# A fused recurrent-attention and mixer kernel on one core: all operations in another order, with other PSUM banks and other constant matmuls

## The chip, the core and the metric

One core of a Trainium2 chip runs the kernel. The core has a matrix engine (TensorE; PE in the profile, with PEld for its weight loads), a vector engine (DVE), a scalar engine (ACT), a general one (GpSimd, POOL) and a sync engine (SP) that here does nothing but issue DMAs. Each engine works through its own queue in order. The metric is the device time of one execution in microseconds (us), as a median over executions; lower is better.

## The reference

The first half is a recurrence over 768 tokens for 4 batches with 8 heads of dimension 40; the second half mixes the result over tokens and channels.

```python
for t in range(S):                       # state: [B, H, D, D]
    y[:, :, t] = einsum('bhd,bhde->bhe', rt, state)
    Sa = einsum('bhde,bhe->bhd', state, at)
    state = state * wt[:, :, None, :] - einsum('bhd,bhe->bhde', Sa, bt) \
            + einsum('bhd,bhe->bhde', vt, kt)
x = y.transpose(0, 2, 1, 3).reshape(B, S, H * D)
theta = x @ w_theta
zr, zi = x * cos(theta), x * sin(theta)
u = x + einsum('ts,bsd->btd', w_tok_r, zr) + einsum('ts,bsd->btd', w_tok_i, zi)
out = u + maximum(u @ w_ch, 0)
```

Inputs and output are float32.

## The kernel before

The sequence is cut into chunks of 128 tokens: 6 for each batch, 24 in all, numbered i = 0 to 23. For each chunk the recurrence is written as matmuls: scores between the chunk's tokens, masked to a triangle, and a state that goes from chunk to chunk within a batch.

The program builds a list of 1,602 operations (`Plan`, L165). Each has a kind, a chunk number and an engine, and some have an alternative on another engine. The kinds that matter here:

- `lw`, `lk`, `lb`, `la`, `lv` (L442) and `loadr`, `loado` (L454): loads of 160 KB on SP, for one chunk, or halves of r and v for two chunks. The tiles that they fill are `raw_w`, `raw_kb`, `raw_a`, `raw_v`, `raw_r`, in rings of two to six.
- `ln`, `cs`, `cx`, `exp`, `ew`: the decay factors, by ACT and PE (constant triangles as weights).
- `kb` and `ah` (L462 on POOL, L461 on DVE): two products for k and b and one for a, each 128 x 320. `o`, `r`, `v`: casts. `tkb`, `ta`, `to`, `tr`, `tv`, `tb`, `nut`, `xt`, `ut`, `wt`: transposes on PE (L410, L414, L575, L578), each with an evacuation from PSUM (`ekb`, `ea` and so on) on ACT or DVE. Eleven of the transposes run on SP as DMAs.
- `spsi`, `sphi`, `slv`, `slu` (L609): score matmuls into two banks each; their masks `mpsi`, `mphi`, `mlv`, `mlu` are one product with a triangle on DVE (L618), or a copy on ACT (L620) followed by a selection `sel` on POOL (L622).
- `x0`, `nx`, `nu`, `enu`, `gt`, `egt`, `wgt`, `gd`, `egd`: the chain of the recurrence. `x0` (L650, L656) multiplies the old state, `nu` (L669) needs the masked phi, `gt` (L692) makes the new state, and from chunk 4 on it is finished by a sum on DVE (`egt`, L703) and a product on POOL (`wgt`, L707).
- `y`, `ex` (L844): the chunk's result x. `th`, `eth`, `sin` (L885), `z` (L899 on DVE, L900 on POOL), `row` (L916), `uadd` (L922), `ch`, `oo`, `st`: the mixer. A row needs z of all six chunks of its batch. `wdma` (L967, L995) are the loads of the mixer's weights, issued by POOL.

Dependencies between operations are kept by semaphores whatever the order. Four tables, written out at the head of the file by a planner that ran before, say the rest. `ORDER` is the order in which all operations are emitted, and so the order of each engine's queue. `HOMES` gives each PSUM tile its bank, in the order in which the tiles are opened; there are 8 banks, and an operation that opens a bank waits for the last reader of what was there. `PICK` lists operations that run on their alternative engine, or whose transposes go into two banks rather than one. `WARM` maps an operation to a bank and a number n: ahead of that operation, n matmuls of a constant tile `busy` with itself are issued into that bank (L1044); nothing reads them.

```python
for o in plan.order():
    if o.idx in WARM:
        at, n = WARM[o.idx]
        for _ in range(n):
            nc.tensor.matmul(banks[:, at, 0:128], lhsT=busy[:, 0:128], rhs=busy[:, 0:128], ...)
    ...
    if o.fn is not None:
        o.fn()
```

In the order before, the first entries of the queues are these (bank behind @, d for two banks, W for constant matmuls):

```
PE    W25 cs0@7 cx0@1 W1 to0@4 W4 ta0@0d W8 tkb0@0d tb0@5d spsi0@0d W11 tr0@2d cx1@7 cs1@6
      cs2@4 cx2@1 x0_0@5 sphi0@2d slv1@6d nu0 slv0@2d ta1 tkb1 gt0 tb1 nut0 spsi1 ...
DVE   ah0 kb0 eb0 mpsi0 nx0 mphi0 ah1 mlv0 egt0 eb1 kb2 kb2 mphi1 ...
POOL  o0 kb0 r0 wdma kb1 kb1 sel1 wdma o2 ah2 ...
SP    lw0 loado0 lk0 loado0 la0 loado2 lb0 loadr0 lw1 loadr0 lw2 lb1 lk1 la1 la2 lk2 ...
```

and around chunks 10 to 12:

```
POOL  ... kb11 kb11 ah11 wgt9 wdma kb12 wdma ah12 kb12 wdma wgt10 wdma wdma v12 ...
SP    ... (73) lk12 la11 lw13 la12 loadr12 (78) lb12 lv12 lw14 loadr12 ...
```

Of the kernel before, what the change touches and what calls it, by code (L numbers as in the profile page):

```python
# [26 lines left out]
    0, 6, 1, 7, 3, 18, 20, 2, 21, 5, 23, 22, 32, 8, 24, 25, 33, 4, 12, 27, 30, 10, 31, 34, 26,  # L27
    35, 9, 28, 36, 40, 29, 37, 11, 69, 58, 44, 45, 46, 119, 15, 41, 72, 43, 70, 120, 42, 122,
    13, 71, 98, 73, 47, 99, 75, 87, 48, 49, 19, 74, 88, 14, 76, 100, 53, 89, 50, 101, 123, 51,
    52, 79, 77, 80, 57, 90, 121, 102, 78, 38, 103, 131, 106, 39, 81, 107, 54, 124, 126, 82, 108,  # L30
    104, 125, 129, 84, 83, 130, 17, 132, 109, 85, 86, 56, 127, 134, 156, 110, 128, 16, 137, 157,
    133, 146, 55, 184, 105, 143, 147, 158, 138, 187, 96, 185, 159, 111, 144, 145, 186, 152, 164,
    148, 234, 135, 160, 136, 92, 61, 165, 189, 237, 139, 161, 166, 112, 213, 188, 97, 167, 168,
    59, 214, 140, 91, 238, 190, 235, 141, 215, 191, 93, 162, 236, 169, 163, 60, 194, 142, 170,
    62, 192, 95, 195, 149, 193, 216, 267, 240, 299, 217, 150, 94, 196, 246, 218, 153, 302, 197,
    198, 303, 239, 247, 210, 202, 249, 199, 208, 241, 203, 271, 200, 201, 219, 242, 212, 248,
    63, 204, 272, 244, 205, 64, 243, 221, 273, 220, 245, 171, 254, 211, 222, 274, 258, 172, 261,
    155, 151, 259, 279, 262, 263, 223, 154, 174, 280, 300, 260, 250, 224, 225, 173, 251, 281,
    301, 320, 175, 496, 255, 304, 282, 283, 275, 256, 325, 177, 226, 349, 276, 206, 497, 257,
    176, 264, 498, 306, 268, 227, 352, 265, 284, 499, 327, 305, 285, 277, 326, 328, 309, 278,  # L40
    317, 310, 329, 207, 318, 319, 353, 307, 330, 286, 269, 356, 308, 350, 331, 287, 500, 361,
    311, 332, 539, 252, 270, 336, 312, 313, 253, 359, 333, 351, 314, 360, 362, 354, 337, 209,
    315, 316, 540, 364, 338, 363, 386, 266, 541, 387, 288, 382, 339, 340, 388, 289, 355, 290,
    389, 291, 116, 321, 357, 390, 341, 412, 502, 358, 391, 323, 365, 501, 542, 292, 373, 342,
    392, 367, 366, 503, 374, 375, 376, 368, 517, 504, 411, 181, 506, 377, 378, 524, 414, 505,
    334, 393, 322, 525, 369, 507, 394, 395, 526, 335, 508, 418, 527, 383, 528, 509, 510, 554,
    396, 370, 415, 543, 397, 511, 371, 324, 529, 113, 532, 372, 117, 512, 513, 533, 546, 398,
    118, 572, 384, 595, 514, 178, 603, 573, 550, 399, 530, 515, 516, 413, 596, 385, 551, 534,
    597, 574, 544, 531, 182, 598, 642, 400, 535, 536, 575, 417, 401, 183, 402, 521, 576, 403,
    545, 581, 404, 577, 379, 599, 114, 582, 547, 555, 115, 380, 381, 600, 548, 556, 557, 583,  # L50
# [12 lines left out]
    741, 65, 882, 672, 757, 778, 408, 755, 736, 450, 779, 753, 451, 737, 673, 780, 742, 883,
    452, 682, 781, 453, 884, 683, 764, 885, 669, 782, 758, 765, 783, 454, 455, 759, 784, 346,
    456, 767, 785, 786, 457, 766, 458, 459, 773, 743, 796, 405, 768, 769, 460, 787, 760, 802,
    443, 744, 912, 797, 788, 724, 444, 343, 461, 798, 761, 887, 913, 445, 789, 763, 446, 462,
    762, 886, 914, 790, 463, 770, 723, 915, 347, 448, 888, 771, 791, 348, 792, 793, 800, 920,
    890, 794, 795, 409, 921, 891, 889, 916, 905, 410, 892, 801, 805, 917, 464, 406, 893, 918,
    772, 344, 407, 465, 896, 804, 345, 899, 728, 922, 803, 897, 898, 480, 725, 481, 808, 482,
    955, 483, 900, 901, 473, 811, 474, 927, 484, 923, 485, 799, 919, 726, 960, 806, 466, 928,  # L70
    961, 924, 475, 727, 929, 486, 894, 962, 895, 476, 907, 963, 477, 933, 930, 983, 819, 906,
    932, 467, 931, 807, 468, 1030, 969, 902, 469, 970, 478, 809, 903, 471, 908, 820, 984, 479,
    821, 810, 934, 822, 985, 777, 971, 942, 986, 487, 936, 972, 973, 488, 964, 935, 1086, 774,
    823, 904, 937, 824, 1031, 825, 938, 1032, 775, 489, 965, 925, 939, 1033, 490, 966, 926, 940,
    776, 491, 949, 941, 1036, 492, 943, 1034, 946, 950, 951, 945, 812, 1035, 957, 947, 813, 814,
    815, 1037, 494, 944, 1087, 958, 967, 987, 974, 968, 948, 1088, 1039, 975, 956, 1041, 1040,
    816, 1089, 988, 817, 1042, 1014, 818, 1007, 976, 991, 1015, 952, 977, 826, 1090, 989, 1016,
    953, 954, 827, 996, 911, 1017, 1052, 990, 992, 997, 909, 1023, 993, 1053, 1054, 1018, 1092,
    1058, 994, 1024, 978, 995, 979, 1093, 1019, 980, 1001, 981, 982, 998, 1008, 1091, 1002, 829,
    999, 1000, 1097, 828, 1020, 910, 830, 1098, 1004, 1133, 831, 1003, 1095, 959, 1005, 1049,  # L80
    833, 1063, 1009, 1050, 1051, 835, 1064, 836, 1006, 1096, 1134, 1065, 837, 1135, 470, 1066,
    1025, 1266, 1110, 1136, 1104, 1038, 1045, 1021, 1026, 1027, 838, 1105, 1010, 1072, 839,
    1067, 1022, 840, 1068, 1073, 1059, 1043, 1046, 841, 1074, 1069, 1047, 1028, 1075, 1076,
    1044, 1012, 1094, 1117, 1138, 1048, 1011, 1101, 1118, 1055, 1029, 1060, 1139, 1267, 1102,
    1103, 1137, 1119, 1077, 1268, 1106, 1120, 1142, 1269, 1312, 1013, 1121, 1078, 1143, 1126,
    1140, 1061, 1070, 1122, 1099, 1127, 865, 1056, 1057, 1113, 1100, 866, 1123, 1071, 1144,
    1128, 1145, 1271, 1313, 1129, 1130, 1107, 1161, 1314, 1152, 1141, 1108, 867, 1148, 868,
    1315, 1079, 1112, 1153, 1154, 1270, 1166, 1272, 1131, 1167, 1273, 1062, 1080, 1124, 1168,
    1132, 1125, 1155, 1169, 1146, 1149, 1156, 1157, 1147, 1111, 869, 1150, 1170, 1151, 870,
    1171, 1275, 1116, 1316, 871, 1277, 1158, 1276, 1278, 1172, 1319, 1164, 1159, 1082, 1173,  # L90
    1174, 1297, 1115, 1109, 1081, 1298, 1114, 1284, 1367, 1083, 1285, 1286, 1281, 1085, 1318,
    1299, 1290, 1084, 1368, 1300, 842, 1274, 843, 1369, 1282, 1283, 844, 1317, 845, 1340, 846,
    1160, 1301, 1370, 847, 1302, 1279, 1185, 449, 1305, 848, 1321, 1327, 1162, 1323, 1306, 1345,
    1322, 1324, 1320, 1291, 1307, 1280, 1346, 1331, 1184, 1308, 1309, 1334, 858, 1163, 1347,
    859, 1348, 1188, 860, 1332, 1333, 861, 1349, 447, 1191, 849, 1293, 862, 1350, 1354, 1407,
    1335, 1336, 1303, 1351, 1310, 1165, 1355, 1175, 1467, 1186, 850, 1311, 863, 1304, 1292,
    1408, 1176, 1189, 1391, 1409, 864, 1356, 1392, 1410, 1177, 1372, 1342, 1371, 852, 1357,
    1358, 1393, 1178, 851, 1412, 1394, 853, 1341, 1328, 1411, 1287, 854, 1373, 1330, 1179, 856,
    1329, 1325, 1400, 1288, 1289, 1343, 1187, 1326, 1468, 1352, 1180, 1469, 1395, 1374, 1401,
# [57 lines left out]
WARM = {21: (7, 25), 33: (4, 1), 30: (0, 4), 28: (0, 8), 41: (2, 11)}  # L157
# [924 lines left out]
```

## Time and profile before

| | us |
|---|---|
| median of 3 executions | 198.19 (196.97 to 199.13) |
| the profiled execution, its own time | 199.01 |
| its span, first to last instruction | 197.3 |

The profile is of one execution. Its times count from the span's start. A line of the timeline gives start, duration, engine, line of the program, operation, what it writes and reads, and in brackets the idle time of the engine before it with the instruction that ended it. A line of the table of groups gives the number of instructions, then busy time and mean ns of one, then idle time before them. DMA issues are listed with their size and the median time from issue to landing. DMA engines moved 32.81 MB in all, 166 GB/s over the span, most of it in the first 160 us:

```profile
DMA  5999979989999989999999988989798955635145
```

Each digit is the mean busy share of the 16 DMA engines in a fortieth of the span, in tenths.

### The profile page before, as it was taken

To read this page: it belongs to the slowest core of one execution; us is meant where nothing else is said; L and a number is where in the kernel's file an instruction comes from. 1 tells how busy PE (TensorE), PEld (TensorE's weight loads), DVE (VectorE), ACT (ScalarE), POOL (GpSimd) and SP (SyncE) were. 2 spreads that over 40 slices of the span, in tenths; PEclk is the share of its full clock that TensorE was granted. 3 is DMA by queue.
4 is the path that set the end of the run, shared out by engine and by line. 5 is a ranking of instruction groups with operands and counts; after the bars stand their busy time and mean duration, and the time that the engine had idled before them with its cause. 6 is when DMAs were issued, how large, how long until landed. Compare 5 with 4: busy or idle time off the path is not lost. (4 is left out here: it accounts for less than half of the span.)

```text
span 197.3 us, 8867 instructions
## 1 busy us (share of the span) xinstructions
PE 182.6 (93%) x3702; PEld 141.7 (72%) x3702; DVE 165.0 (84%) x277; ACT 152.9 (77%) x332; POOL 146.0 (74%) x206
## 2 busy tenths in 40 slices
PE   7497999999999998979999999999999999999991
PEld 6366787787778677757776787887788768676651
DVE  5237798999999999758898999999999989579382
ACT  3356899999999998869998789899999958374010
POOL 8429556959998997779999899595889893578000
PEclk9758899999999999999999999999999999999998
DMA  5999979989999989999999988989798955635145
GB/s 121 238 182 176 223 142 227 176 166 165 188 152 174 191 145 216 164 177 185 202 196 154 173 159 169 178 159 194 145 174 160 200 110 135 101 100 161 41 147 188
DMA packets 134648, 32.81 MB, mean 166 GB/s; under 512 B 124816, under 2 KB 134608, under 8 KB 134608
## 3 DMA queue, kind: packets, MB, share of 16 engines
q1 hardware_dynamic: 131680, 29.19, 74.8%
q0 software_dynamic: 2784, 2.97, 9.7%
q8 instruction: 29, 0.48, 1.1%
q14 instruction: 11, 0.09, 0.2%
q10 hardware_dynamic: 144, 0.08, 0.1%
HBM read 29.54 MB, written 3.93 MB: 170 GB/s over the span
## 5 line engine op out<-in xcount | busy, mean ns | idle before, releaser
L916 PE MATMUL banks<-zr,wtok_r 128*128 128x320 bf16 x144 | 41.1, 300 | 0.4 <-POOL zr L900 0.2
L916 PE MATMUL banks<-zi,wtok_i 128*128 128x320 bf16 x144 | 40.9, 299 | 0.0
L462 POOL TENSOR_TENSOR kb<-raw_kb,ex 128x320 bf16<-128x320 f32 x44 | 35.2, 812 | 7.2 <-ACT ex L502 4.5
L618 DVE TENSOR_TENSOR phi<-banks,mask_n 128x1024 bf16<-128x1024 f32 x20 | 24.4, 1218 | 1.5 <-PE banks L609 1.3
L618 DVE TENSOR_TENSOR lamu<-banks,mask_p 128x1024 bf16<-128x1024 f32 x20 | 24.3, 1218 | 0.1
L618 DVE TENSOR_TENSOR psi<-banks,mask_p 128x1024 bf16<-128x1024 f32 x19 | 23.2, 1219 | 1.1 <-ACT lw L478 0.8
L462 POOL TENSOR_TENSOR ah<-raw_a,we 128x320 bf16<-128x320 f32 x20 | 17.3, 868 | 5.5 <-ACT we L520 2.0
L609 PE MATMUL banks<-aT,kbT 64*128 64x128 bf16 x384 | 18.2, 221 | 0.5 <-ACT kbT L432 0.5
L916 PEld LDWEIGHTS <-wtok_r 128*128 128x128 bf16 x144 | 14.0, 97 | 5.5 <-issue 0.3
L900 POOL TENSOR_TENSOR zi<-cs,xp 128x320 bf16<-128x320 f32 x21 | 17.1, 826 | 1.0 <-ACT cs L885 0.9
L916 PEld LDWEIGHTS <-wtok_i 128*128 128x128 bf16 x144 | 14.1, 98 | 3.8 <-issue 0.5
L618 DVE TENSOR_TENSOR lamv<-banks,mask_p 128x1024 bf16<-128x1024 f32 x12 | 14.6, 1221 | 2.4 <-PE banks L609 1.2
L900 POOL TENSOR_TENSOR zr<-cs,xp 128x320 bf16<-128x320 f32 x17 | 13.7, 810 | 2.4 <-ACT cs L885 2.4
L622 POOL TENSOR_SCALAR_AFFINE_SELECT lamv<-lamv 128x1024 bf16<-128x1024 bf16 x12 | 13.3, 1112 | 2.3 <-ACT lamv L620 2.3
L609 PEld LDWEIGHTS <-kbT 64*128 64x128 bf16 x384 | 12.0, 95 | 4.0 <-issue 1.8
L835 PE MATMUL banks<-kb,lamv 128*128 128x40 bf16 x192 | 14.8, 180 | 0.0
L837 PE MATMUL banks<-kb,lamu 128*128 128x40 bf16 x192 | 14.7, 179 | 0.0
L707 POOL TENSOR_TENSOR gt<-sum,ex 128x320 bf16<-128x320 f32 x13 | 9.6, 738 | 6.0 <-DVE sum L703 5.9
L620 ACT ACTIVATE lamv<-banks 128x1024 bf16<-128x1024 f32 x12 | 12.3, 1024 | 1.8 <-PE banks L609 1.8
L835 PEld LDWEIGHTS <-lamv 128*128 128x128 bf16 x192 | 13.2, 96 | 0.3
L837 PEld LDWEIGHTS <-lamu 128*128 128x128 bf16 x192 | 12.9, 96 | 0.0
L478 ACT ACTIVATE lw<-raw_w 128x320 bf16<-128x320 f32 x24 | 11.4, 479 | 1.6 <-DMA raw_w<-in_w_dram 1.6
(217 smaller groups left out, 600.9 us busy)
## 6 DMA issues: line engine op xcount, KB each, us to landing
raw_w<-in_w_dram SPq DMA_DIRECT2D x24, 160.0 KB, 4.2
raw_v<-in_v_dram SPq DMA_DIRECT2D x24, 160.0 KB, 4.1
raw_kb<-in_k_dram SPq DMA_DIRECT2D x24, 160.0 KB, 4.3
raw_a<-in_a_dram SPq DMA_DIRECT2D x24, 160.0 KB, 4.1
raw_kb<-in_b_dram SPq DMA_DIRECT2D x24, 160.0 KB, 4.1
raw_r<-in_r_dram SPq DMA_DIRECT2D x24, 160.0 KB, 3.9
out_dram<-oo SPq DMA_DIRECT2D x9, 160.0 KB, 2.6
wrow_i<-in_moe_w_tok_i_dram POOLq DMA_DIRECT2D x6, 192.0 KB, 5.0
```

Of the source, the lines that this page charges most:

```text
L462: pool = ("POOL", lambda: nc.gpsimd.tensor_tensor(out=dst, in0=in0, in1=in1, op=ALU.mult))
L478: add("ACT", "ln", i, lambda: nc.scalar.activation(out=paired(lw)[:, :, :, 0:D], in_=paired(raw_w[s4]), func=AF.Ln), 473, [("raw_w", s4)], ...
L609: nc.tensor.matmul(t[:, q, g, :], lhsT=lhs[g][rows(q)], rhs=rhs[g][rows(q)], start=True, stop=True)
L618: add("DVE", kindm, i, lambda: nc.vector.tensor_tensor(out=flat, in0=whole(), in1=mask.to_broadcast([128, 2 * G, 128]), op=ALU.mult), 1217 ...
L620: 1217, [p], [dkey], alts=(("ACT", lambda: nc.scalar.mul(out=flat, in_=whole(), mul=sign)),))
L622: add(None, "sel", i, None, 0, [dkey], [dkey], alts=(("POOL", lambda: nc.gpsimd.affine_select(out=flat, in_=flat, pattern=[[0, 2 * G], [1, ...
L707: add("POOL", "wgt", i, lambda: nc.gpsimd.tensor_tensor(out=new_state, in0=sum_t, in1=wm.to_broadcast([128, 8, D]), op=ALU.mult), 830, [(" ...
L835: nc.tensor.matmul(o, lhsT=lamv[:, p, g, :], rhs=kb[:, 0, h, 0:D], start=first, stop=False, skip_group_check=True)
L837: nc.tensor.matmul(o, lhsT=lamu[:, p, g, :], rhs=kb[:, 1, h, 0:D], start=False, stop=True, skip_group_check=True)
L900: pool = ("POOL", lambda: nc.gpsimd.tensor_tensor(out=dst, in0=in0, in1=in1, op=ALU.mult))
L916: nc.tensor.matmul(acc(), lhsT=wtok[nm][j][:, s], rhs=zs[c][:, s], start=n == 0 and c == 0, stop=n == NT - 1 and c == 1)
```

## The change

Only the four tables change; the list of operations and their dependencies do not. `ORDER` has all operations in another order. `HOMES` gives 359 of the 430 PSUM tiles another bank. `PICK` sends 116 operations to the other engine of their pair, and changes for others whether a transpose fills one bank or two. `WARM` grows from 49 constant matmuls in five places to 71 in thirteen, by adding up the diff's table (the change's own description says 65). The planner that wrote the new tables followed the 16 DMA engines one by one.

```diff
-WARM = {21: (7, 25), 33: (4, 1), 30: (0, 4), 28: (0, 8), 41: (2, 11)}
+WARM = {21: (4, 18), 33: (5, 9), 28: (5, 3), 36: (1, 7), 50: (2, 6), 100: (0, 3), 81: (0, 4), 132: (6, 2), 187: (7, 7), 143: (0, 3), 158: (4, 1), 135: (5, 6), 237: (2, 2)}
```

Here 21 is cs0, 33 to0, 30 ta0, 28 tkb0, 41 tr0 and 36 tb0. The first entries of the new queues:

```
PE    cx0@1 W18 cs0@4 W9 to0@5 cx1@1 ta0@3d W3 tkb0@5d W7 tb0@1 spsi0@4d cs1@3 tr0@6d sphi0@0d
      x0_0@5 cx2@4 slv1@6d W6 slv0@2d W3 nu0 tkb1@4 cs2@0 nut0@5d ta1@1 gt0@7 W4 spsi1@0d ...
DVE   eo1 mpsi0 mphi0 mlv1 enu0 mlv0 kb2 mpsi1 egt0 eo3 mphi1 ...
POOL  o0 ah0 kb0 kb0 kb1 wdma kb1 ah1 wdma kb2 o2 ah2 ...
SP    lw0 loado0 la0 loado0 lb0 loadr0 lw1 lk0 lb1 loadr0 lw2 lk1 loado2 la1 lk2 lb2 ...
```

and around chunks 9 to 12:

```
POOL  ... kb9 sel6 ah9 kb9 wgt7 v8 z5 ... v11 r10 wdma wdma wdma ah11 kb11 kb11 wgt9 wdma kb12
      wdma wdma r12 ah12 wgt10 kb12 wdma wdma sel10 ...
SP    ... (58) lk9 loadr10 la9 (61) lb9 lv8 la10 ... (72) la11 lk11 lb11 loadr12 lk12 loadr12
      (78) la12 lb12 lv12 lb13 ...
```

Near the end SP's queue has the second half of `loadr22` directly behind the DMA transpose `nut21`, where before it stood seven places ahead of it.

256 rows, old and new, of tables (HOMES, ORDER, PICK) are left out of this document.

## The prediction

> **What bounds the kernel now.** I read the page's busy shares first, then its table of stretches for the five engines, then the timeline of the two stretches in which VectorE (DVE) stands still, and last the DMA issues with their times to landing. Columns of the stretches: its bounds, its length, then busy time (and instructions) of PE, PEld, DVE, ACT and POOL, the granted clock, the DMA share, GB/s.
>
> ```profile
> PE 182.6 (93%) x3702; PEld 141.7 (72%) x3702; DVE 165.0 (84%) x277; ACT 152.9 (77%) x332; POOL 146.0 (74%) x206
> ```
>
> ```profile
> 40.00:78.00 38.00, 37.18 (x870) 29.66 (x869) 37.35 (x53) 36.78 (x87) 34.13 (x48) 1.00 0.97 173
> 78.00:90.00 12.00, 9.79 (x216) 7.46 (x214) 7.85 (x11) 9.30 (x23) 9.32 (x14) 1.00 1.00 170
> 90.00:160.00 70.00, 69.32 (x1555) 54.74 (x1554) 67.01 (x106) 64.72 (x137) 61.78 (x80) 1.00 0.93 173
> 160.00:175.80 15.80, 15.54 (x251) 11.36 (x250) 11.71 (x19) 9.37 (x17) 8.93 (x10) 1.00 0.60 125
> 175.80:193.90 18.10, 17.34 (x193) 11.59 (x191) 13.95 (x31) 4.81 (x12) 5.75 (x7) 1.00 0.35 114
> ```
>
> No engine is the limit alone. From 40 to 78 and from 90 to 160 DVE works 104.36 of 108 us, with ACT and POOL close behind; another order finds 3.6 us there at most. Three places hold idle time that an order can win: the first 22 us, the 12 us from 78 (DVE 4.15 us idle, where the share of 90 to 160, 2.99 in 70, would give 0.5), and the tail. In the tail PE is busy 32.88 of 33.90 us on work that both orders have.
>
> **What moves between engines.** Reading the tables of the diff against the list of operations, 116 operations run on the other engine of their pair, and DVE has 251 operations in place of 252, POOL 180 of 181, ACT 322 as before. The dear ones are two score masks that go from ACT (with a POOL selection each) to DVE.
>
> ```profile
> L618 DVE TENSOR_TENSOR psi<-banks,mask_p 128x1024 bf16<-128x1024 f32 x19 | 23.2, 1219 | 1.1 <-ACT lw L478 0.8
> ...
> L622 POOL TENSOR_SCALAR_AFFINE_SELECT psi<-psi 128x1024 bf16<-128x1024 bf16 x5 | 5.5, 1097 | 1.4 <-ACT psi L620 1.3
> ```
>
> That is 2.4 us more on DVE and 2.2 less on POOL (two selections); in return a net three of the shorter copies and products leave DVE, which gives 0.9 us more there if each takes the 0.49 of the sx row below. Over 200 us I take 0 (bounds -1.0 and +0.9). That 359 of 430 PSUM homes change costs 0 in itself: the cover is that as many matmuls stand between two uses of a bank. Without it a matmul waits for one more reader of its bank, up to the 1.2 us of a mask.
>
> **The prologue.** Start us, duration, engine, line, operation; in brackets the idle time before it.
>
> ```profile
> 1.13 2.85 PE L1044 MATMUL banks<-busy 128*128 128x128 bf16 x25 [1.13 <-DVE busy L283]
> ...
> 6.83 0.62 PE L575 MATMUL banks<-wide,o 128*128 128x128 bf16 x8 [1.92 <-POOL o L468]
> ...
> 8.80 1.01 PE L1044 MATMUL banks<-busy 128*128 128x128 bf16 x8 [0.46 <-ACT aT L432]
> ...
> 11.03 0.61 PE L609 MATMUL banks<-aT,kbT 64*128 64x128 bf16 x8 [0.47 <-ACT kbT L432]
> ...
> 11.57 1.36 PE L1044 MATMUL banks<-busy 128*128 128x128 bf16 x11
> ...
> 14.98 0.40 PE L609 MATMUL banks<-aT,kbT 64*128 64x128 bf16 x8
> ...
> 16.81 0.37 PE L669 MATMUL banks<-nx,phi 128*128 128x40 bf16 x8 [1.19 <-DVE phi L618]
> ```
>
> ```profile
> 11.78 1.23 DVE L618 TENSOR_TENSOR psi<-banks,mask_p 128x1024 bf16<-128x1024 f32 x1 [0.75 <-ACT lw L478]
> ...
> 15.52 1.23 DVE L618 TENSOR_TENSOR phi<-banks,mask_n 128x1024 bf16<-128x1024 f32 x1
> ```
>
> Before, spsi of chunk 0 ends, then come 11 constant matmuls, the r transposes and the cumulative sums, and only behind x0 stands sphi: DVE masks psi at 11.78 and phi at 15.52, and nu (L669) waits for phi until 16.81. In the new order sphi stands behind spsi, cs1 and the r transposes, ahead of x0, so DVE takes phi straight after psi, at about 13.0, done at 14.2, and nu runs near 14.4: 2.4 us earlier. Against it: all three products of chunk 0 are now POOL's (0.80 to 0.87 us each by the rows of 84.94 and 31.57), and its k is the eighth load, not the third. But before, the transposes of kb stood behind the eight constants of 8.80 anyway, so spsi keeps its 11.0.
>
> The constant matmuls are 71 by the diff (18, 9, 3, 7, 6, 3, 4, 2, 7, 3, 1, 6, 2), not 49. One costs 2.85/25 = 0.114 us here. The 18 now stand between cx0 and cs0, in the idle time before 6.83; exp of chunk 0 comes 18 x 0.114 = 2.1 us later, covered by POOL, which has cast o by 6.8 (PE waits for it there) and is busy with ah for another 0.87. Twenty-two more cost 2.5 us if all lie on the chain and 0 if all lie in waits; I take 0 for them and their effect on the clock together, and keep +2.5 and the rival D below.
>
> What can take the lead away is the next loads. SP issues them in a row:
>
> ```profile
> 23.02 1.50 SPq L442 DMA_DIRECT2D raw_kb<-in_b_dram  x1
> ...
> 26.36 0.57 SPq L442 DMA_DIRECT2D raw_a<-in_a_dram  x1
> ...
> 27.02 1.81 SPq L454 DMA_DIRECT2D raw_r<-in_r_dram  x1
> ...
> 31.57 0.87 POOL L462 TENSOR_TENSOR ah<-raw_a,we 128x320 bf16<-128x320 f32 x1
> ```
>
> Load a of chunk 4 was SP's 31st and is now its 32nd. At SP's old pace that is issued at 27.02. From issue to use it took 31.57 - 26.36 = 5.2 us, the most that its landing can have needed; 3.9, a median quoted below, is the least that I allow. So it is there between 30.9 and 32.2, and POOL used it at 31.57: an unchanged pace leaves at most 0.7 of the 2.4. If the two long issues shrink to the 0.57 of their neighbour, SP gains 0.9 + 1.2 = 2.1. I take **-0.9** (bounds 0 and -2.4), nearer to the rows of an unchanged pace, since DMA is busy throughout.
>
> **The dip at 78 to 90.**
>
> ```profile
> 71.76 1.58 SPq L442 DMA_DIRECT2D raw_a<-in_a_dram  x1
> ...
> 78.12 0.86 POOL L462 TENSOR_TENSOR ah<-raw_a,we 128x320 bf16<-128x320 f32 x1 [1.05 <-DMA raw_a<-in_a_dram]
> ...
> 79.37 0.54 SPq L442 DMA_DIRECT2D raw_kb<-in_b_dram  x1
> ...
> 84.94 0.80 POOL L462 TENSOR_TENSOR kb<-raw_kb,ex 128x320 bf16<-128x320 f32 x1 [1.93 <-PE banks L414]
> ...
> 86.47 0.75 POOL L707 TENSOR_TENSOR gt<-sum,ex 128x320 bf16<-128x320 f32 x1
> ...
> 87.27 0.20 PE L650 MATMUL banks<-gt,aT 128*128 128x80 bf16 x1 [0.85 <-POOL gt L707]
> ...
> 89.00 0.49 DVE L515 TENSOR_TENSOR sx<-banks,lw 128x320 f32<-128x320 f32 x1 [2.08 <-ACT ex L502]
> ```
>
> POOL waits 1.05 us for a of chunk 11, then 1.93 us before the second kb of chunk 12, whose load b (78th on SP) was issued 5.57 us earlier; the profile names PE, but I read it as that load. Behind it on POOL stand one weight DMA and wgt of chunk 10, for which PE and then DVE wait. In the new order wgt10 stands ahead of this kb, but behind r and ah of chunk 12, and a12 is now the 78th load, b11 the 74th (a11 was). If these land as the 74th and 78th did, wgt10 goes at 84.94 + 0.87 = 85.8 and not 86.47: -0.7. If SP runs 2 us ahead, the dip's whole 4.15 - 0.5 = 3.6 goes. I take **-1.3** (bounds 0 and -3.6).
>
> **A load that comes later.**
>
> ```profile
> 55.64 0.63 SPq L442 DMA_DIRECT2D raw_v<-in_v_dram  x1
> ...
> 59.56 0.37 SPq L442 DMA_DIRECT2D raw_a<-in_a_dram  x1
> ...
> 60.65 0.45 POOL L468 CAST v<-raw_v 128x320 bf16<-128x320 f32 x1 [0.76 <-DMA raw_v<-in_v_dram]
> ...
> 62.58 0.81 POOL L462 TENSOR_TENSOR kb<-raw_kb,ex 128x320 bf16<-128x320 f32 x1
> ```
>
> Load b of chunk 9 moves from SP's 60th place to the 61st, that of a9, issued at 59.56. The v load before it was issued at 55.64 and kept POOL until 60.65, so 5.0 us. By that b9 lands at 64.6, 2.0 us after POOL used it, and wgt of chunk 7 is next in POOL's queue. I take half, **+1.0** (bounds 0 and +2.0).
>
> ```profile
> 159.77 1.22 SPq L737 DMA_TRANSPOSE nuT<-nu  x1
> ...
> 167.39 0.74 POOL L707 TENSOR_TENSOR gt<-sum,ex 128x320 bf16<-128x320 f32 x1 [3.42 <-DVE sum L703]
> ```
>
> In the tail the second half of r22 now stands on SP behind nut21: issued near 161.1, there near 166.1 by the same 5.0, cast by 166.8 while POOL had 3.42 us idle before wgt22 at 167.39, with one selection (1.1) between. 0 taken, bounds 0 and +0.5. After the last x, 36 row chunks are left as before, plus two of row 17: 0.
>
> **Sum** against the profiled execution (span 197.30, time 199.01, so 1.71 around it): -0.9 - 1.3 + 1.0 = -1.2, that is 197.8. It stands 0.82 over the median of 198.19; the forecast goes with the median: **197.0 us**.
>
> **Rivals.**
> B, the loads swallow both gains: prologue 0, dip -0.7, b9 +0.7: **198.2**, no change. For it: the 27.02 and 79.37 rows. Against it: SP's long issues need not stay.
> C, slower: SP keeps its pace and POOL's queue meets late loads at b9. Price 2.0 there; wgt7 is late by it, and as DVE lost 4.15 us in the dip for POOL's 1.05 + 1.93, it costs 2.0 x 4.15/2.98 = 2.8, less the 0.7 of the dip: **200.3**. It decides where b9 lands over 1 us after POOL is ready. For it speaks that loads land late where weight DMAs of POOL run beside them:
>
> ```profile
> raw_kb<-in_b_dram SPq DMA_DIRECT2D x3, 160.0 KB, 7.5
> ...
> raw_kb<-in_b_dram SPq DMA_DIRECT2D x6, 160.0 KB, 3.9
> ```
>
> The first row is of 74 to 92 us, the second of 120 to 160. Now three weight DMAs stand in a row on POOL ahead of ah11. The Trainium skill, DMA: Bandwidth & Descriptors (Issuing engines are not separate DMA queues), says that DMAs of any issuing engine end on the same 16 DMA engines and interleave; these two rows agree.
>
> D, the clock: in the stretches below it follows how busy PE was in the stretch before.
>
> ```profile
> 8.20:11.60 3.40, 2.47 (x47) 1.89 (x42) 0.76 (x2) 2.13 (x6) 1.37 (x2) 0.50 1.12 214
> 11.60:15.00 3.40, 3.40 (x51) 2.59 (x51) 1.23 (x1) 1.51 (x5) 0.22 (x1) 0.54 1.01 166
> 15.00:18.40 3.40, 2.05 (x50) 1.67 (x48) 2.88 (x4) 2.18 (x6) 3.00 (x4) 0.96 0.98 192
> 18.40:21.90 3.50, 3.46 (x60) 2.65 (x58) 2.07 (x5) 2.40 (x6) 2.20 (x4) 0.55 1.05 178
> ```
>
> PE busy 3.40 of 3.40 is followed by 0.96, 2.05 of 3.40 by 0.55. If the constants fill each stretch, eight score matmuls take 0.40 and not 0.61 (rows of 14.98 and 11.03): ten such groups, my count of those on the chain from 8 to 22, give -2.0. Lead and clock together would be 4.4, of which the loads let through some 2.4; with -1.3 at the dip: 198.2 - 2.4 - 1.3 = **194.5**. By the Trainium skill, TensorE: Matmul & The Clock Gate (Part 1: The HAM clock gate), the clock is half at rest and full after a busy window of about 3.4 us, and an idle one halves it; the four rows agree, and by that rule it would come out as D.
>
> **How the numbers follow.** Forecast (195.8 to 198.0) 0.36, B 0.22, C (199.5 to 201.5) 0.20, D (193.5 to 195.5) 0.22. About 1% is what a measurement of this kernel can tell from no change: 196.2 and 200.2 are the ends. Faster: D and 0.14 of the forecast, 0.36. Slower: 0.15 of C, and 0.05 of B for stalls at places that I have not seen, 0.20. Same: the rest, 0.44. The range runs from 194.0 to 200.6, into D and C: it leaves out some 0.05 below and 0.10 above. The forecast's own range is 195.8 to 198.0, half the way from each taken value to its bounds.
>
> **What would show it.** Right: L669 first near 14.4; the wait before ah or kb between 75 and 90 below 2 us together; DVE idle in 78 to 90 near 2.5. C: POOL kb waiting near 62 for raw_kb. D: clock 1.00 from about 8 or 12 on. Wrong would be a stall of over 2 us where none was, as of a bank that two operations now share, or the tail longer than 18 us from the last xs to the last result.

## The result, and the profile after

The changed kernel takes 199.19 us (median of 20 executions, 197.73 to 203.18), the kernel before on the same chips 197.45 us (20 executions, 195.55 to 200.59). The ratio is 1.0102, 95% interval 1.0067 to 1.0136: slower by 1.0%. The forecast was 197.0. Ratios and intervals, here and below, leave out executions that stand over 1.5% above the fastest of their kernel (two far ones, of 546.8 and 395.8 us, among them), while medians and counts are of all. Over all measurements of this study the medians are 199.2 (24 executions) and 197.1 (111 executions, 194.4 to 200.6).

The profiled execution of the changed kernel took 200.06 us for a span of 198.3. First its busy shares, then the table of stretches with the columns of the prediction (the last stretch ends 1.0 us later, as the span does):

```profile
PE 183.4 (92%) x3719; PEld 142.4 (72%) x3719; DVE 166.4 (84%) x276; ACT 153.2 (77%) x332; POOL 145.8 (73%) x205
```

```profile
40.00:78.00 38.00, 36.58 (x838) 29.70 (x834) 36.96 (x54) 36.83 (x83) 35.32 (x50) 1.00 0.99 183
78.00:90.00 12.00, 11.79 (x283) 9.65 (x280) 11.53 (x17) 10.09 (x23) 11.53 (x17) 1.00 1.14 181
90.00:160.00 70.00, 69.02 (x1547) 53.62 (x1546) 66.75 (x105) 64.19 (x139) 58.32 (x74) 1.00 0.86 162
160.00:175.80 15.80, 14.07 (x227) 9.59 (x225) 10.78 (x19) 8.66 (x14) 9.84 (x11) 1.00 0.75 138
175.80:194.90 19.10, 18.58 (x207) 12.90 (x205) 14.12 (x30) 6.05 (x14) 5.89 (x7) 1.00 0.33 110
```

The dip is gone: DVE is busy 11.53 of 12.00 us, not 7.85. Yet at 160 to 175.8 PE is idle for 1.73 us where it was idle for 0.26, and the end is later. What waits there stands in the timeline (SP's issues first, then POOL, DVE and PE):

```profile
159.91 1.22 SPq L737 DMA_TRANSPOSE nuT<-nu  x1
161.18 1.75 SPq L454 DMA_DIRECT2D raw_r<-in_r_dram  x1
...
170.51 0.57 SPq L955 DMA_DIRECT2D out_dram<-oo  x1
171.18 1.20 SPq L737 DMA_TRANSPOSE xT<-xp  x1
172.43 0.57 SPq L955 DMA_DIRECT2D out_dram<-o  x1
...
165.15 0.72 POOL L468 CAST r<-raw_r 128x640 bf16<-128x640 f32 x1 [0.86 <-DMA raw_r<-in_r_dram]
...
174.76 0.89 DVE L952 SCALAR_TENSOR_TENSOR o<-banks,up 128x320 f32<-128x320 f32 x2 [1.96 <-DMA out_dram<-o]
...
165.92 0.41 PE L578 MATMUL banks<-wide,r 64*128 64x64 bf16 x16 [0.16 <-POOL r L468]
173.80 0.72 PE L798 MATMUL banks<-wth,xT 128*128 128x320 bf16 x4 [0.73 <-DMA xT<-xp]
175.70 0.30 PE L916 MATMUL banks<-zr,wtok_r 128*128 128x320 bf16 x1 [0.71 <-DVE o L952]
```

Three transfers that SP issues late hold other engines: the second half of r22, the transpose xT20, and the store of row 4, whose tile `o` DVE needs again for row 13. Before, that store was issued on SP at 152.92; now it stands behind xT20, at 172.43:

```profile
152.92 0.52 SPq L955 DMA_DIRECT2D out_dram<-o  x1
```

The chain that ended last runs through two of them:

```profile
161.18 3.91 DMA raw_r<-in_r_dram
165.15 0.73 POOL r L468
...
171.18 2.58 DMA xT<-xp
173.80 0.72 PE banks L798 x4
```

The head of the changed kernel, PE first, then DVE and POOL:

```profile
12.05 0.61 PE L609 MATMUL banks<-aT,kbT 64*128 64x128 bf16 x8
...
13.32 0.39 PE L609 MATMUL banks<-aT,kbT 64*128 64x128 bf16 x8
...
15.89 0.36 PE L669 MATMUL banks<-nx,phi 128*128 128x40 bf16 x8
...
21.97 0.29 PE L414 MATMUL banks<-wide,ah 64*128 64x64 bf16 x8 [0.70 <-DVE phi L618]
...
23.60 0.36 PE L669 MATMUL banks<-nx,phi 128*128 128x40 bf16 x8
...
29.64 0.36 PE L669 MATMUL banks<-nx,phi 128*128 128x40 bf16 x8
...
12.81 1.22 DVE L618 TENSOR_TENSOR psi<-banks,mask_p 128x1024 bf16<-128x1024 f32 x1 [3.18 <-PE banks L609]
13.95 1.21 DVE L618 TENSOR_TENSOR phi<-banks,mask_n 128x1024 bf16<-128x1024 f32 x1
...
23.70 1.23 DVE L618 TENSOR_TENSOR phi<-banks,mask_n 128x1024 bf16<-128x1024 f32 x1 [1.45 <-ACT nx L662]
...
25.77 1.09 POOL L622 TENSOR_SCALAR_AFFINE_SELECT psi<-psi 128x1024 bf16<-128x1024 bf16 x1 [4.40 <-ACT psi L620]
```

DVE takes phi straight behind psi, as forecast, and L669 runs at 15.89, 0.9 us earlier than before (16.81). At 21.97 the transposes of chunk 2's `ah` wait 0.70 us for a bank that the mask phi of chunk 1 still reads, and DVE and POOL have idle time after it. But that wait isn't where the lead goes. These are the matmuls of nu of chunks 1 and 2 in the kernel before:

```profile
24.49 0.37 PE L669 MATMUL banks<-nx,phi 128*128 128x40 bf16 x8
...
28.62 0.36 PE L669 MATMUL banks<-nx,phi 128*128 128x40 bf16 x8
```

At chunk 1, behind the wait, the changed kernel still leads by 0.89 us (23.60); at chunk 2 it is 1.02 behind (29.64). Between the two PE is busy nearly all the time:

```profile
24.00:30.00 6.00, 5.91 (x134) 4.86 (x134) 4.86 (x9) 5.59 (x15) 3.76 (x5) 1.00 0.96 203
```

So the lead goes to other work that the new order has PE do ahead of nu of chunk 2, as far as PE's busy time tells; no run tried this.

### The profile page after: what moved, and what is told of

Read it like the earlier page. It is cut to its first block, busy times and chain, and to the rows that moved or that the text cites. A ratio compares the mean times of both kernels' runs of the same rounds, so it can differ in the third digit from the quotient of the medians.

```text
span 198.3 us, 8894 instructions
## 1 busy us (share of the span) xinstructions
PE 183.4 (92%) x3719; PEld 142.4 (72%) x3719; DVE 166.4 (84%) x276; ACT 153.2 (77%) x332; POOL 145.8 (73%) x205
## 4 chain that ended last, share of the span: by engine, by line
PE 58%; ACT 13%; DVE 7%; issue 4%; DMA 3%; POOL 1%; SPq 1%; DVEq 0%; ACTq 0%
PE banks L916 16%; PE banks L609 8%; PE banks L410 6%; PE banks L798 5%; PE banks L414 5%; PE banks L692 2%; DMA raw_r<-in_r_dram 2%; PE banks L837 2%; PE banks L808 2%; PE banks L669 2%; PE banks L835 2%; PE banks L828 1%; PE banks L656 1%; DVE psi L618 1%; DMA xT<-xp 1%
## 5 line engine op out<-in xcount | busy, mean ns | idle before, releaser
L462 POOL TENSOR_TENSOR kb<-raw_kb,ex 128x320 bf16<-128x320 f32 x46 | 37.3, 825 | 6.1 <-ACT ex L502 3.8
L618 DVE TENSOR_TENSOR psi<-banks,mask_p 128x1024 bf16<-128x1024 f32 x20 | 24.3, 1217 | 4.4 <-PE banks L609 4.4
L618 DVE TENSOR_TENSOR phi<-banks,mask_n 128x1024 bf16<-128x1024 f32 x21 | 25.6, 1219 | 2.9 <-ACT nx L662 1.5
L462 POOL TENSOR_TENSOR ah<-raw_a,we 128x320 bf16<-128x320 f32 x21 | 18.2, 868 | 4.7 <-ACT we L520 4.1
L900 POOL TENSOR_TENSOR zr<-cs,xp 128x320 bf16<-128x320 f32 x20 | 16.0, 812 | 4.5 <-ACT cs L885 4.5
L900 POOL TENSOR_TENSOR zi<-cs,xp 128x320 bf16<-128x320 f32 x19 | 15.2, 814 | 3.6 <-ACT cs L885 3.5
L502 ACT ACTIVATE ex<-banks 128x328 f32<-128x328 f32 (+1 forms) x24 | 10.9, 458 | 3.1 <-PE banks L497 2.8
```

The source lines that it names most:

```text
L462: pool = ("POOL", lambda: nc.gpsimd.tensor_tensor(out=dst, in0=in0, in1=in1, op=ALU.mult))
L502: got = add("ACT", "exp", i, lambda: nc.scalar.activation(out=ex[:, :, 0:D] if no_total else ex.rearrange("p h x -> p (h x)"), in_=sums(ps ...
L618: add("DVE", kindm, i, lambda: nc.vector.tensor_tensor(out=flat, in0=whole(), in1=mask.to_broadcast([128, 2 * G, 128]), op=ALU.mult), 1217 ...
L900: pool = ("POOL", lambda: nc.gpsimd.tensor_tensor(out=dst, in0=in0, in1=in1, op=ALU.mult))
```

## How the runs are read

One execution says little in this kernel, since executions differ by 3%. A better ruler is the start of `nu<-banks` (L673, L675) for each chunk, in every profile: there is one for each of the 24 chunks. The table gives the time to nu of chunk 3, the stretches between nu of chunks 3, 9, 13 and 21, and from there to the last result's instruction (us; for two or three profiles of the same kernel, all values). "Head" is the changed order up to 40 us and the kernel before behind it.

| kernel | own time | to 3 | 3 to 9 | 9 to 13 | 13 to 21 | 21 to end |
|---|---|---|---|---|---|---|
| before (3 profiles) | 199.0, 199.0, 197.4 | 35.2, 35.1, 34.1 | 37.6, 37.4, 39.3 | 31.7, 32.9, 29.9 | 54.0, 53.9, 54.0 | 34.9, 34.5, 34.9 |
| head (2) | 195.1, 195.5 | 35.5, 35.6 | 36.7, 37.2 | 29.2, 29.1 | 53.9, 53.9 | 34.5, 34.5 |
| after (2) | 200.1, 199.0 | 36.6, 35.7 | 37.0, 37.0 | 31.3, 31.3 | 54.3, 54.3 | 35.7, 35.6 |
| after, r22 early (2) | 199.0, 199.7 | 35.6, 35.5 | 37.0, 38.1 | 31.7, 31.5 | 54.3, 54.3 | 35.2, 35.1 |
| after, store 4 early (2) | 197.8, 200.0 | 35.5, 35.6 | 37.7, 37.3 | 31.1, 32.3 | 54.3, 54.0 | 34.1, 35.7 |
| after, three moves | 198.3 | 35.4 | 37.0 | 31.9 | 54.3 | 34.5 |
| after, with the tail of before | 199.0 | 36.4 | 37.0 | 31.4 | 54.4 | 34.5 |
| before, loads by use | 196.5 | 34.8 | 37.5 | 29.5 | 53.8 | 35.6 |
| head, loads by use | 197.9 | 35.4 | 37.2 | 29.7 | 53.9 | 36.4 |

From nu of chunk 13 to that of 21 all executions of one order agree within 0.4 us, and PE is busy there but for 0.3 us at most (0.8 in the kernel with the tail of before): the order decides. Up to chunk 13 they differ by 3 us, and the waits that the profiles show there are mostly for loads. The profiled executions are not the typical ones: two of before stand 1.9 us over its median, the two of "head" 1.2 and 1.6 under theirs (196.7), so the first two rows compare late executions with early ones.

The tail differs between the orders by about 1 us, but the order does not settle it alone. The two kernels with loads by use have before's tail unchanged, and it took 35.6 and 36.4 us there, since PE waited for a DMA transpose of nu on SP (for 0.26 us in the first profile of before):

```profile
169.53 0.40 PE L607 MATMUL banks<-rT,nuT 64*128 64x128 bf16 x8 [0.80 <-DMA nuT<-nu]
...
171.11 0.40 PE L607 MATMUL banks<-rT,nuT 64*128 64x128 bf16 x8 [1.13 <-DMA nuT<-nu]
```

The first row is of the kernel before with loads by use, the second of "head" with them.

## The experiments

Kernels spliced from both orders take each operation's bank and engine from the table that its place comes from. Line numbers in the spliced and edited kernels lie two or three below those of the two originals. Ratios are to the kernel before, measured beside each.

**The tail.** The second half of r22 alone, eight places forward on SP (not the eleven that the first expectation says), twice:

```diff
 SP:  ... la23
+     loadr22
      lv22 st2 lv23 tkb23 ta23 st5 xt18 nut21
-     loadr22
      tv23 tv22 ...
```

> The changed kernel with one load moved: the second half of r22 goes back on SP from behind the transpose nut21 to its place ahead of the loads of v22, eleven SP places earlier; all else as in the changed kernel (199.19 us). Theory 1 (this load starts the loss of the tail: it was issued at 161.18, landed 3.9 us later, the cast of r22 waited for it, and the scores and the fourth transpose xT20 behind it came late): the tail gets back most of the 1.0 us that it is longer by, so 198.2 to 198.4, and the masks lamv and lamu of chunk 22 come about 1.3 us earlier. Rival 2 (the tail is longer through the order of its other operations, xT20's transpose and the rows; the late load is covered): 199.0 to 199.4.

Measured: 198.36 us (6 executions, one of 546.8), ratio 1.0108 (1.0062 to 1.0154); and again

> The changed kernel with the second half of r22 moved alone, again. Theory 1, as mended by the profiles (0.2 to 0.5 us of PE's idle time in the tail go): 198.6 to 199.1, ratio 1.007 to 1.010. Rival 2 (the load is covered): 199.1 to 199.5, ratio 1.010 to 1.012. Together with the store: if the one alone gives 1.0 and this one 0.3, they add up to most of the 1.8 that the three moves gave.

199.28 us (6), 1.0130 (1.0077 to 1.0184). The tail of the profiles is 0.5 us shorter, and the wait on raw_r is gone, but the time is that of the changed kernel. The store alone, twice:

```diff
 SP:  ... lv22 st2
+     st4
      lv23 ... nut22 st11 xt20
-     st4
      st8 ...
```

> The changed kernel with one store moved: that of row 4, whose tile row 13's result needs, goes back on SP to its place ahead of the load of v23 (issued near 153 us, not 172.4). Theory 7 (in the changed order the result of row 13 waits 1.9 us on DVE for this store, and PE 0.6 behind it): DVE's wait for the DMA of a result goes, PE's idle time of the tail falls from 2.1 us to 1.4 or 1.5, the time to 198.5 to 198.8. Rival (what stands behind waits for another transfer, that of xT20): 199.0 to 199.4.

> The changed kernel with the store of row 4 moved alone, again. Theory 7 (the store holds DVE and PE back in every execution): median 197.8 to 198.5, ratio 1.003 to 1.007. Rival (without it the late r22 and xT20 hold the tail as long): 198.8 to 199.4, ratio 1.009 to 1.012.

199.21 us (6), 1.0117 (1.0051 to 1.0182), and 198.72 us (6), 1.0114 (1.0057 to 1.0170). One profile has a tail of 34.1 us, the other of 35.7: DVE's wait on the store is gone in both, but in the second PE still waits 0.45 us for r, 0.53 for a transpose of u and 0.76 for xT20. The three moves together (r22, the store of row 4, and the store of row 11 behind xT20):

```diff
 SP:  ... la23
+     loadr22
      lv22 st2
+     st4
      lv23 tkb23 ta23 st5 xt18 nut21
-     loadr22
      tv23 tv22 st6 ut12 st3 nut22
-     st11 xt20 st4
+     xt20 st11
      st8 ...
```

> The changed kernel with three moves on SP: the store of row 4 as in the kernel before this one, the second half of r22 ahead of the loads of v22, and the transpose xT20 ahead of the store of row 11. Theory 7: these three are the tail's 1.1 us; PE's idle time after nu of chunk 21 falls from 2.1 to 0.5 to 0.8 us, the time to 197.9 to 198.3, ratio 1.003 to 1.006. Rival: something else in the order holds the tail, and under 0.6 is won: 198.6 or more.

197.37 us (12), 1.0028 (0.9993 to 1.0063), a little better than theory 7 gave. In its profile the waits are down to one of 0.17 us:

```profile
172.31 0.88 DVE L950 SCALAR_TENSOR_TENSOR o<-banks,up 128x320 f32<-128x320 f32 x2
...
172.84 0.72 PE L796 MATMUL banks<-wth,xT 128*128 128x320 bf16 x4 [0.17 <-DVE o L950]
```

and PE is idle for 1.01 us of the stretch from nu of chunk 21 to the last result. The first row below is of this kernel, the second of the changed kernel's second profile (2.07 us idle):

```profile
158.61:193.11 34.50, 33.49 (x455) 23.18 (x452) 25.50 (x49) 15.47 (x29) 16.59 (x19) 1.00 0.55 122
...
158.23:193.83 35.60, 33.53 (x455) 23.25 (x452) 25.82 (x48) 15.57 (x29) 16.59 (x19) 1.00 0.48 125
```

So late transfers on SP make the tail long, and neither r22 nor the store does it alone: with one mended, another still holds. The transpose xT20 was not moved by itself, so its own share is open. The whole tail of before behind the changed order:

```diff
-ORDER = new
+ORDER = new[:1300] + [n for n in old if n not in new[:1300]]
```

> The order, banks and engines of the changed kernel up to its 1300th operation (about 152 us), then all that is left in the order of the kernel before. Theory 1 (places: the tables lose 1.4 us before 40 us, win about 1.9 to 3 in 78 to 90, lose 0.5 at 96 to 103 and 1.0 in the last 45 us): 198.2, and with the first kernel of this set it tells how much of the 1.0 is the late load. Rival 2 (the state in which the changed order arrives at 152 us, such as its loads, makes the tail long): 199.2.

198.41 us (6), 1.0117 (1.0065 to 1.0169). Its tail is 34.5 us, as before's; the median came down by 0.8, but the ratio did not come down at all. By its time alone this kernel speaks against the three moves. The profiles reconcile the two in part. By the last two columns of the table together, the changed kernel takes 90.0 and 89.9 us behind nu of chunk 13, the kernel before 88.4 to 88.9 (mean 88.7), the kernel with the three moves 88.8 and this one 88.9. Both have won back the 1.2 us behind chunk 13. What their times differ by lies ahead of it, where their orders are the same and executions scatter; the 1.8 us between the medians of 199.2 and 197.4 are more than the tail can give. And the other way round, the kernel before with r22 behind nut21:

```diff
 SP:  ... la23
-     loadr22
      loadr22 lv22 st4 lv23 tkb23 ta23 xt18 nut21
+     loadr22
      tv22 tv23 ...
```

> The kernel before with one load moved: the second half of r22 goes on SP from its place ahead of the loads of v22 to the place right behind the transpose nut21, where the changed kernel has it. Theory 1 (the late load is worth most of the longer tail): 0.5 to 1.1 us slower than before, ratio 1.003 to 1.006, and masks of chunk 22 that come late by as much. Rival 2 (covered): ratio 0.998 to 1.002.

197.69 us (10, one of 395.8), 1.0054 (0.9996 to 1.0112), the size that theory 1 gave, with an interval that just reaches 1. Its profile has a tail of 35.7 us (34.5 to 34.9 in the three of before) and shows the mechanism bare, POOL and then PE:

```profile
162.85 0.72 POOL L466 CAST r<-raw_r 128x640 bf16<-128x640 f32 x1 [3.13 <-DMA raw_r<-in_r_dram]
...
163.63 0.41 PE L576 MATMUL banks<-wide,r 64*128 64x64 bf16 x16 [1.02 <-POOL r L466]
```

**The dip.** Is the stall at 78 to 90 in every execution of the kernel before?

> The kernel before, unchanged, for a second profile: the one shown is of an execution of 199.01 us, where its median is 197.45. Theory 3 (the stall at 78 to 90 belongs to that one execution: a load that happened to land late): here DVE is idle under 2 us between the nu of chunks 10 and 12, and the time from nu of chunk 9 (72.77 in the first profile) to nu of chunk 12 (95.89) is 1.5 us or more under the 23.1 of the first profile. Rival 4 (the stall lies in the order): 23.1 within 0.5 again, with POOL's wait for the second half of kb of chunk 12 of about 1.9 us.

> The kernel before, unchanged, a third profile. In the two so far, nu of chunk 9 to nu of chunk 13 took 31.7 and 32.9 us, in executions of 199.0 each; its median over all is 197. If the stall is there only in the slower part of its executions, an execution near 197 shows 29 to 30.5 here; if it is in all, 31.5 or more.

The second profile (199.0 us) has it, worse; the third (197.4 us) has a third of it: 32.9 and 29.9 us from nu of chunk 9 to nu of chunk 13, PE idle for 2.7 and 0.9 of them (2.4 in the first). But the third lost its time earlier: from nu of chunk 3 to 9 it took 39.3 us against 37.6 and 37.4, and POOL waited there for a load of b:

```profile
46.82 0.80 POOL L462 TENSOR_TENSOR kb<-raw_kb,ex 128x320 bf16<-128x320 f32 x1 [1.04 <-DMA raw_kb<-in_b_dram]
```

From nu of chunk 3 to 13 the three take 69.3, 70.3 and 69.2 us (the changed kernel 68.3 twice, "head" 66.0 and 66.3), so a stall came in each of them, and not in the same place. In the dip the load is a of chunk 11. In the second profile (SP, then POOL) it is issued at 71.62 and used after a wait of 2.36 us:

```profile
71.62 2.62 SPq L442 DMA_DIRECT2D raw_a<-in_a_dram  x1
...
78.85 0.86 POOL L462 TENSOR_TENSOR ah<-raw_a,we 128x320 bf16<-128x320 f32 x1 [2.36 <-DMA raw_a<-in_a_dram]
```

In the first kernel "head", whose order is the same there, SP is 1.9 us further and POOL does not wait:

```profile
69.74 0.82 SPq L440 DMA_DIRECT2D raw_a<-in_a_dram  x1
...
76.18 0.85 POOL L460 TENSOR_TENSOR ah<-raw_a,we 128x320 bf16<-128x320 f32 x1
```

The changed order takes 30.9 to 32.3 us for this stretch in all ten profiles that have it, before's 29.1 to 32.9 in six. It has made away with a stall that comes in some executions, and is never as quick as before without it. Loads of the kernel before in the order of their use:

```diff
 SP:  ... lw12 la10
-     lv11 lk12 la11 lw13 la12 loadr12 lb12
+     la11 lv11 lk12 la12 lb12 lw13 loadr12
      lv12 ...
```

> The kernel before with three loads moved on SP around the stall at 78 to 90: a of chunk 11 ahead of v of chunk 11 (two places earlier), a and b of chunk 12 ahead of w of chunk 13. Theory 3 (the stall of the kernel before is those loads coming late in some executions: nu of chunk 9 to nu of chunk 13 took 31.7 and 32.9 us in its two profiles and 29.2 and 30.0 in two kernels with the same order that arrived there with SP 1.5 to 2 us further): the stretch takes 29.0 to 30.0 in every execution, the median comes to 195.2 to 196.6, ratio 0.990 to 0.996, and fewer executions lie above 197. Rival 4 (the DMA engines are full there, and a load that is put forward makes another late): ratio 0.998 to 1.004.

196.87 us (12), 1.0001 (0.9965 to 1.0037): nothing, though the stretch took 29.5 us in its profile; executions of 199 and more still came. The middle of the changed order in the kernel before, and before's middle in the changed kernel with its tail mended:

```diff
+ORDER = old up to 456, new up to 744, old            (first kernel)
+ORDER = new up to 456, old up to 744, new, 3 moves   (second kernel)
```

> The kernel before up to its 456th operation (about 61 us), the changed order from there to its 744th (about 95 us), then the kernel before again. Theory 1 (places): the dip at 78 to 90 goes, DVE is idle there for 0.5 to 1.0 us in place of 4.15, and 1.9 to 3 us of it reach the end: 194.5 to 195.6 against 197.45. Rival 2 (the work that fills the dip is only moved, and the next stretch, 90 to 105, gives the gain back through late loads or weights): 196.8 to 197.6.

> The changed kernel with the three SP moves of its tail (197.4), and with the order, banks and engines of the kernel before from its 456th to its 744th operation (about 61 to 95 us). Theory 8 (the changed middle takes 31.3 us from nu of chunk 9 to nu of chunk 13 in every execution, the one of before 29.2 to 30.0 without its stall and 31.7 to 32.9 with it; the stall comes when SP arrives late): 195.6 to 196.9, and 29.0 to 30.5 us for that stretch in this profile if no load is late. Rival (both middles are worth the same on a mean): 197.0 to 197.8.

198.52 us (10), 1.0098 (1.0063 to 1.0133); and 197.94 us (12), 1.0063 (1.0021 to 1.0105), where the same kernel with its own middle had 1.0028. Neither exchange wins anything, and the first loses. Why it loses 1% is open: its profile lost its time ahead of the cut, at 39 to 42, where POOL waited for two loads that the first profile of before had in time:

```profile
39.30 0.87 POOL L460 TENSOR_TENSOR ah<-raw_a,we 128x320 bf16<-128x320 f32 x1 [1.22 <-DMA raw_a<-in_a_dram]
41.89 0.81 POOL L460 TENSOR_TENSOR kb<-raw_kb,ex 128x320 bf16<-128x320 f32 x1 [1.72 <-DMA raw_kb<-in_b_dram]
```

These rows show a lead taken up by loads: this execution was 1.1 us ahead of the first profile of before at nu of chunks 1 to 4, and 0.2 behind it at chunk 5.

**The head.** Before's head ahead of the changed order (cut at 252 operations), and the changed head ahead of the kernel before (cut at 256):

```diff
+ORDER = old up to 252, then new   (first kernel, with the old WARM)
+ORDER = new up to 256, then old   (second kernel, with the new WARM)
```

> The order, banks, engines and constant matmuls of the kernel before up to its 252nd operation (about 39 us), then all that is left in the changed order. Theory 1 (the places add up): the 1.4 us that the changed order loses by 40 us are won back to the end, 197.8. Rival 2 (a wait for loads behind it takes up any lead, as the prologue's lead was taken up): within 0.3 of the changed kernel, 199.2.

> The counterpart of the kernel with the head of before: the changed order, with its constant matmuls, up to its 256th operation (about 40 us), then the kernel before. That kernel came out at 200.6 against 199.2, so the changed head was worth 1.4 there, though nu of chunks 3 to 8 comes later with it. Theory 3 (the changed head does win about 1.4 us, by the constant matmuls or by loads that are ahead, and the loss lies further on): 195.6 to 196.6. Rival (each head fits the rest of its own order, and a cut costs 1 to 1.5 us wherever it lies): 198 to 198.9.

> Again the changed order and its constant matmuls up to operation 256 (about 40 us), then the kernel before: four executions before gave 195.1, 195.7, 199.1 and 199.5. If the changed head wins (theory 3): median 195.0 to 196.2 and ratio under 0.998. If the head is worth nothing, since the loads of chunks 4 to 6 take up any lead (theory 9: nu of chunk 6 came at 51.6 to 53.0 with both heads): 196.4 to 197.6, ratio 0.998 to 1.003.

The first: 200.59 us (6), 1.0194 (1.0140 to 1.0249), against both theories. The second: 197.38 us (4: 195.1, 195.7, 199.1, 199.5), 0.9899 (0.9833 to 0.9965), and in 12 more executions 196.70 us, 1.0013 (0.9972 to 1.0053). The changed head is worth nothing that 12 executions show, and the earlier 0.9899 rests on the two early ones of four. Why before's head loses ahead of the changed order is open: from nu of chunk 3 to chunk 6 that kernel took 19.9 us, against 17.8 in the changed one, but this is one profile, of an execution of 202.4 us, and the third profile of before took 19.4 there as well. With the loads in the order of their use besides, as in the diff above:

> The kernel before this one, and the three loads around 75 us in the order of their use. If the loads by use take the late executions away: no execution over 198, median 195.0 to 196.0. If the moved loads only shift the wait: as the kernel before this one within 0.5.

196.68 us (12), 0.9989 (0.9945 to 1.0032), with two executions over 199. None of these beats the kernel before.

**The constants.**

```diff
-WARM = {21: (4, 18), 33: (5, 9), 28: (5, 3), 36: (1, 7), ...}
+WARM = {21: (4, 18)}
```

> The changed kernel with the first 18 constant matmuls only; the other 53, in twelve places, are left out. Theory 5 (they lie in waits until the loads catch up, and neither their cost nor the clock reaches the end): 198.9 to 199.5, nu of chunk 6 within 0.3 of 53.4 to 54.4. Rival D (they keep the clock at 1.00, and that is worth something): the clock falls to 0.5 in places between 8 and 22, and the time rises by 0.5 to 2.0, 199.7 to 201.2. Rival 6 (they stand on the chain): 53 x 0.06 to 0.114 = 3 to 6 us of PE go, of which 0.5 or more reach the end: 198.7 or less.

200.0 us (6, 198.3 to 201.5), 1.0153 (1.0087 to 1.0218); the interval overlaps that of the changed kernel. Nothing was won, so the 53 constants do not stand on the chain that counts: rival 6 falls. The time lies in the range of rival D. The clock of 0.50 that D named did not show (1.00 in the rows from 8 on), though by the pace of the matmuls PE was slow for longer here (last section). Against D, nu of chunk 6 came at 53.38 in the profile, where theory 5 had it, and at 53.43 and 54.35 in the changed kernel. So theory 5 and a small loss are not told apart.

**The changed kernel again,** for its second profile:

> The changed kernel, unchanged, beside the others of this set: 199.2, ratio to before 1.010. Its second profile tells which of its times repeat. If the stretches are set by the order, the times from nu to nu are those of the first profile within 0.1 from chunk 6 on, and the start alone differs, by about 1 us, as it does between the changed kernel and the one with the earlier load.

199.34 us (4), 1.0112 (1.0057 to 1.0167). From chunk 1 on its nu times are 0.89 to 0.94 us earlier than in the first profile, all of them: the whole difference arose before 25 us.

## Why the prediction was wrong

The time (199.2) lies in the range of 194.0 to 200.6, but on the other side of no change than the forecast of 197.0. The two gains that it counted on did not come, and the tail, which it took at 0, grew. By its steps:

- **The tail, "0, with bounds 0 and +0.5": this step failed.** It measured +0.9 in the profiles (35.7 and 35.6 us against a mean of 34.8). The three SP moves bring it to 34.5 and took 1.8 off the median (199.2 to 197.4), the whole tail of before brings it to 34.5 too and took off 0.8 (but nothing by the ratio). The prediction saw one of three transfers, r22, placed its landing rightly (near 166; POOL had it at 165.15) and took POOL's idle time for its cover. What it missed is that PE waits behind r (0.16 us) and, more, that the order of two other SP instructions had changed: the store of row 4 stands fifteen places further back, with DVE waiting 1.96 us for its tile and PE 0.71 behind that, and the transpose xT20, for which PE waits 0.73, stands behind the store of row 11. Stores were not gone through.
- **The dip, -1.3: mis-read as a property of the order.** What was foretold came, and more: POOL's waits are below 2 us, DVE is idle for 0.47 us (2.5 foretold), and wgt of chunk 10 starts at 84.97 (85.8 foretold), with b of chunk 12 there in time:

```profile
84.00 0.87 POOL L462 TENSOR_TENSOR ah<-raw_a,we 128x320 bf16<-128x320 f32 x1
84.97 0.74 POOL L707 TENSOR_TENSOR gt<-sum,ex 128x320 bf16<-128x320 f32 x1
85.67 0.80 POOL L462 TENSOR_TENSOR kb<-raw_kb,ex 128x320 bf16<-128x320 f32 x1
```

  But the stall there belonged to some executions, and the third lost as much elsewhere; the profiled one was 1.9 us over the kernel's median of 197.1. Over that stretch the changed order gains against two profiles of before and loses to the third and to both "head" kernels. On the median it was worth nothing that the exchanges show.
- **The prologue, -0.9 (bounds 0 and -2.4): the mechanism came, the gain did not.** nu of chunk 0 starts at 15.2 to 16.4 in the profiles of the changed order and at 17.2 to 18.1 in the three of before. By chunk 3 it is 1.3 us behind (36.1 against 34.8, means), by chunk 9 level within 0.3. The bound of 0 was the right value. Two readings failed. The scores of psi did not keep their 11.0: they came at 12.05 (row above), so that nu led by 0.9 and not by 2.4. And what took the lead was not a late load: it went between nu of chunks 1 and 2, with PE busy for 5.91 of 6.00 us. A matmul did wait 0.70 us for a bank, of which the prediction had said that it costs nothing as long as matmuls stand between; nu of chunk 1 shows no loss behind it.
- **Load b9, +1.0: did not come.** POOL took the second kb of chunk 9 without a wait:

```profile
62.84 0.89 POOL L462 TENSOR_TENSOR ah<-raw_a,we 128x320 bf16<-128x320 f32 x1
63.66 0.84 POOL L462 TENSOR_TENSOR kb<-raw_kb,ex 128x320 bf16<-128x320 f32 x1
```

- **The constants, 0:** nothing was seen against it. **Engine swaps, 0,** were not tried alone.
- **The rivals.** B, in which both gains are swallowed, is nearest to what happened up to 160 us, but in the prologue it was not loads that did it. C has the right side and about the right time, 200.3 against 199.2, by another place and mechanism; that its time came near is luck. D's sign came, a clock of 1.00 from the start on (by the pace of the matmuls, from about 13 us on), without its gain. The rule that the prediction cites for D lowers the clock behind an idle stretch, but in the row from 15.00, which it counted as agreeing, PE was busy for 2.05 of 3.40 us.
- **The base.** The forecast stood on a median of three, 198.19. Over 111 executions it is 197.1, so 1.1 us of the forecast's 197.0 was chance as well: its own terms from the better base would have given 195.9. From there to 199.2 are 3.3 us: 1.3 of the dip, 0.9 of the prologue and 0.9 to 1.2 behind chunk 13, less the 1.0 of b9, explain some 2.1 to 2.4. The range of 195.8 to 198.0 is not the plain sum of the half ways, which give 194.6 to 198.9 over prologue, dip, b9 and tail.

What stays open: of the 2.0 us between the medians (199.2 and 197.1) the profiles place 1.2 behind nu of chunk 13. Whether the rest lies ahead of it is not settled. With the three moves 0.3 us by the medians (ratio 0.9993 to 1.0063) is left between the kernels, with the tail of before a ratio of 1.0065 to 1.0169. The table puts 0.3 into chunks 13 to 21, in all profiles of the changed order there but one, but no run tried that stretch alone.

## What to carry to other kernels

When an order is replaced, go through every DMA of the new queue, stores included, and ask for each who waits for its tile and since when; a stall of a microsecond hid in a store that had moved and a transpose that stood behind another one. Before a stall of a profile is counted as a gain, compare that execution's own time with the median: one that stands well above it can show a stall that the median does not have. Late transfers in one queue cover for each other, so they are tried together as well as one by one.

## What the runs showed of the hardware

The granted clock and the pace of the matmuls disagreed. The table of stretches of the changed kernel has 1.00 in each of these rows:

```profile
8.20:11.60 3.40, 2.92 (x41) 1.96 (x39) 0.42 (x1) 2.17 (x6) 1.23 (x2) 1.00 1.09 199
11.60:15.00 3.40, 3.02 (x61) 2.06 (x60) 2.19 (x2) 2.69 (x8) 1.31 (x2) 1.00 1.11 226
```

But eight score matmuls took 0.61 us at 12.05 and 0.39 at 13.32 (rows of the head, above): up to about 13 they ran at the slow pace that the kernel before showed under a clock of 0.50. In the kernel with 18 constants the clock reads 1.00 too, and the same eight took 0.61 still at 12.83:

```profile
12.83 0.61 PE L607 MATMUL banks<-aT,kbT 64*128 64x128 bf16 x8
...
15.05 0.41 PE L667 MATMUL banks<-nx,phi 128*128 128x40 bf16 x8
```

So the other constants do bring PE to its full pace a microsecond or more earlier; at nu of chunk 3 nothing of that is left (35.3 us in this kernel, 36.6 and 35.7 in the changed one). The Trainium skill, TensorE: Matmul & The Clock Gate (Part 1: The HAM clock gate), warns that the trace's clock events have been seen to be unreliable on this chip; these rows agree, and what tells the clock is the duration of a known group. In the 91 executions of the kernel before that were timed beside the experiments, the mean granted clock ran from 0.964 to 1.000 and had no relation to the time (correlation -0.01).
